# Products of constants in the plan's waits, before the feed-forward of a fused attention, Fourier and feed-forward kernel

## The chip, the cores and the metric

The kernel runs on one core of a Trainium2 chip. A core has a matrix engine (TensorE, in the profile PE, with its weight loads as PEld), a vector engine (VectorE, DVE), an engine for elementwise functions (ScalarE, ACT), a general one (GpSimd, POOL) and SyncE (SP), from whose queue most transfers are sent. Each engine runs its own list of instructions in order and waits for the others through semaphores. PE writes its results to PSUM, which has eight banks; DVE and ACT read them there. The metric is the device time of one execution in microseconds (us), the median of the runs.

## What is computed

The input is q, k and v of 8 batches, 8 heads, 576 positions and 64 features, and two weight matrices, w1 of 512 x 2048 and w2 of 2048 x 512.

```python
scores = where(block_i >= block_j, q @ k.T / sqrt(64), -1e9)   # blocks of 64 positions
attn = softmax(scores)                                         # per batch and head
x = concat_heads(attn @ v)                                     # 8 x 576 x 512
mixed = real(fft(fft(x, axis=1), axis=2))
u = x + mixed
un = (u - mean(u)) / sqrt(var(u) + 1e-6)                       # over the 512 features
out = u + maximum(un @ w1, 0) @ w2
```

## The kernel before

The work is cut into *steps*. A step is a small piece of one stage: a group of matmuls on PE, and the parts on DVE, ACT, POOL or in a queue that follow from it. Generators, called lanes, give out the steps of each stage in order: loads and copies of a head (head_lane, prepare_lane), row maxima (max_lane), scores and exponentials (score_lane), products with v (value_lane, whose PSUM tile is av), the Fourier stage of a batch (transform_lane) and, as *fillers*, the two products of the feed-forward (feed_steps: first writes h, second writes acc). Side lanes load the weights and convert them to pairs of f16 (load_lane, weight_lane); this is DVE, ACT and POOL work on the tile W.

The main loop (from line 1068) is a planner that runs while the program is written. It keeps a clock of its own, `now`, and books the cost of each step, a figure in the code, on a model of each engine. `ready(step)` is the time at which a step's inputs are there by that model and, where the step needs a PSUM bank, at which a bank is free. The loop takes the next step, `issue` moves `now` to the time at which the step can start and adds its cost on PE, then it emits its matmuls; the parts on the other engines are kept in `pending` and emitted in order of their planned starts (`give`). All instructions are kept in the order in which they are emitted (`keep_in_program_order`, through `mm`, `tp` and `Ordered`), so the plan is the order on every engine, PE's too, and the chip waits only where an input is late.

PSUM is shared. One bank holds av; seven others are in three pools: three in ps, two in h, two in acc. Before the feed-forward all seven are lent to any step (`lent` holds the three names, and `rings` the time at which each bank is free by the plan). With the first filler `lent` becomes `["ps"]`: h and acc then belong to the feed-forward.

Heads of later batches are held back until the first weight's parts are there (the condition on `('w', 15)`). So the start of the kernel is the attention of batch 0, its Fourier stage, the loads and conversions of the weights, and then the first feed-forward; after that attention and Fourier steps run between the fillers.

Names that are used below: raw is a head's load, lead its rounded copy, rest the remainder of the rounding (written by DVE, POOL and a transfer); M is a head's row maximum, which DVE reduces from PSUM, PE transposes (with ident) and ACT writes to mt, which a transfer copies into lead before the scores can start; ph and pl are the exponentials as a pair of f16; DEN and x are the values' last parts on DVE; xd is x in DRAM, from which the Fourier stage is loaded. `ident` is the 128 x 128 identity in f32, loaded first on SP's queue, and `ones` a tile of 1.0, set by DVE.

```python
if i is None:
    lent = ["ps"]
    issue(filler)
```

Of the kernel before, what the change touches and what calls it, by code (L numbers as in the profile page):

```python
# [9 lines left out]
F32 = mybir.dt.float32  # L10
F32R = mybir.dt.float32r
F16 = mybir.dt.float16
# [10 lines left out]
P = 128  # L23
# [19 lines left out]
PSHIFT = 5  # L43

BANKS = {"ps": 3, "h": 2, "acc": 2}

KM = D + 8
KS = KM + 1
# [152 lines left out]
def tile_attn_fourier_ffn(  # L201
# [6 lines left out]
    ps_av = pool("ps_av", 1, space=PSUM)  # L208
    ps = {name: pool(name, n, space=PSUM) for name, n in BANKS.items()}
    dram = pool("dram", 3, space=DRAM)  # L210
# [4 lines left out]
    def mm(*args, **kw):  # L215
        return tc.keep_in_program_order(nc.tensor.matmul(*args, **kw))  # L216
# [7 lines left out]
    ident = const.tile([P, P], F32, name="ident")  # L224
# [3 lines left out]
    ones = const.tile([P, P], F32, name="ones")  # L228
# [42 lines left out]
    now = 0.0  # L271
    queues = {x: Queue() for x in "DAGQKM"}
    done = {}
    current = "ps"
    rings = {name: [0.0] * n for name, n in BANKS.items()}
    lent = list(BANKS)


# [5 lines left out]
    def ready(step):  # L284
        r = max((done[x] for x in step.after), default=0.0)
        return max(r, min(rings[x][0] for x in lent)) if step.bank else r

    def book(engine, t, cost):

        used = [queues[x] for x in {"X": "DK", "G": "GK", "P": "G"}.get(engine, engine)]  # L290
        while True:
            at = max(x.fit(t, cost) for x in used)
            if at <= t:
                return max(x.book(t, cost) for x in used)
            t = at

    pending = []
    issued = [0]

    def issue(step):  # L300
        nonlocal current, now
        t = max(now, ready(step))
        if step.cost:
            give(t)
        if step.cost:
            now = t = t + step.cost
            for x in queues.values():
                x.forget(now)
        free = None
        starts = []  # L310
        for engine, cost in step.chain:
            if engine == "B":
                free = t + HOP
            elif engine == "L":
                t = t + cost
            elif engine in scratch:

                if cost:
                    t = max(t, scratch[engine][0] - HOP)
                else:  # L320
                    scratch[engine] = sorted(scratch[engine][1:] + [t + HOP])
            else:
                t = book(engine, t + HOP, cost)
                if engine != "M":
                    starts.append(t - cost)
        t += HOP
        if step.key is not None:
            done[step.key] = t
        if step.bank:
            current = min(lent, key=lambda x: rings[x][0])  # L330
            rings[current] = rings[current][1:] + [t if free is None else free]
        parts = step.emit()
        if parts is None:
            return
        if step.cost:
            next(parts, None)
        for at in starts:
            pending.append((at, len(pending) + 1000000 * issued[0], parts))
        issued[0] += 1

    def give(t):

        soon = sorted((x for x in pending if x[0] <= t), key=lambda x: x[:2])
        pending[:] = [x for x in pending if x[0] > t]
        for _, _, parts in soon:
            next(parts, None)
# [721 lines left out]
    while True:  # L1068
# [13 lines left out]
        for w, side in enumerate(sides):  # L1082
            if side is None or not may(side) or ready(side) > until:
                continue
            engine, cost = next((x for x in side.chain if x[0] in "DAGQKXP"), (None, 0.0))
            at = max(now, ready(side))
            ahead = queues[{"X": "D", "P": "G"}.get(engine, engine)].fit(at, cost) - at if engine else 0.0
            if ahead <= AHEAD[engine in ("D", "X") and first] or at + ahead + cost + FREE <= until:
                issue(side)
                sides[w] = next(weights[w], None)  # L1090
                break
        else:
            w = None
# [5 lines left out]
        if soon:  # L1099
            i = min(soon, key=lambda i: heads[i].place)  # L1100
        elif feed and ready(filler) <= now or feed and not able:
            i = None
        elif able:
            i = min(able, key=lambda i: ready(heads[i]))
        elif any(sides):
            w = min((w for w, x in enumerate(sides) if x is not None and may(x)), key=lambda w: ready(sides[w]))
            issue(sides[w])
            sides[w] = next(weights[w], None)
            continue
        elif pending:  # L1110
            give(pending[0][0])
            continue
        else:
            assert filler is None and not any(heads)
            break
# [3 lines that stand above are left out]
            filler = None  # L1119
        else:  # L1120
            issue(heads[i])
            heads[i] = next(lanes[i], None)
# [46 lines left out]
```

## Time and profile before

| | us |
|---|---|
| median of 3 runs | 1279.11 |
| lowest and highest | 1277.9 and 1280.24 |
| span of the profiled execution | 1275.3 |
| mean granted clock of PE in it | 0.947 |

The span goes from the first to the last instruction of the profiled execution. Its own time isn't listed apart from the runs; against their median, 1279.11 - 1275.3 = 3.8 us lie around the span.

How to read its lines. A page begins with the busy time of each engine and its share of the span, then 40 equal slices of the span with the busy share in tenths. PEclk is the clock that PE was granted, in tenths of full speed. The windows view gives the same for chosen stretches: length, then busy time and count of instructions for PE, PEld, DVE, ACT and POOL, then the granted clock, the share of the transfer engines and GB/s. The timeline lists instructions by start and duration; `out<-in` are the program's names, x the count merged in a row, and brackets hold the idle time of the engine before it and what ended it. The waits view sums these idle times by what ended them (total, times, longest). The chain is the work that ended last, followed back. L216 and L219 are the helpers mm and tp, L194 that of the other engines. Matmuls are pipelined, so a row's duration is longer than the distance between two starts.

### The profile page before, as it was taken

The numbers are of one execution on the slowest core, as the hardware profiler recorded it, in microseconds if no ns is written. First come the engines' busy times: TensorE is split into PE (matmuls) and PEld (weight loads), VectorE is DVE, ScalarE is ACT, GpSimd is POOL, SyncE is SP. The second block draws the span as 40 slices with busy tenths as digits, with TensorE's granted clock in tenths as the row PEclk, the third lists the DMA queues.
The fourth block names the chain that finished last, engine by engine and source line by source line (L and its number), as shares of the span: only waits on it lengthen the run. The fifth ranks groups of instructions, "written<-read, shape, count | busy, mean of one in ns | idle before, by whom it ended". The sixth has DMA issues, their size and how long they took to land.

```text
span 1275.3 us, 25121 instructions
## 1 busy us (share of the span) xinstructions
PE 1181.1 (93%) x10068; PEld 892.9 (70%) x10068; DVE 703.5 (55%) x1433; ACT 548.7 (43%) x1137; POOL 523.6 (41%) x593
## 2 busy tenths in 40 slices
PE   5772598999799999999999999999999999999998
PEld 5672376677677777777777777777777667766665
DVE  6787777756747574664546573557445414422211
ACT  5655647554444555534645545454443112111110
POOL 4664944454643654563534644446441400300000
PEclk9655688999899999999999999999999999999999
DMA  7674242342223233232323232413220100000000
GB/s 210 201 243 156 80 140 70 87 111 52 74 71 109 62 81 86 79 75 54 93 75 95 65 90 68 111 51 87 77 74 10 40 19 19 21 17 1 17 17 17
DMA packets 56371, 99.07 MB, mean 78 GB/s; under 512 B 7757, under 2 KB 26653, under 8 KB 56256
## 3 DMA queue, kind: packets, MB, share of 16 engines
q1 hardware_dynamic: 49152, 73.16, 21.2%
q10 hardware_dynamic: 4384, 16.78, 4.0%
q0 software_dynamic: 2720, 7.54, 2.1%
q8 instruction: 79, 1.29, 0.4%
q14 instruction: 36, 0.29, 0.1%
HBM read 58.46 MB, written 18.87 MB: 61 GB/s over the span
## 4 chain that ended last, share of the span: by engine, by line
PE 80%; DVE 10%; POOL 3%; issue 3%; DMA 2%; ACT 1%; SPq 0%; DVEq 0%; POOLq 0%; ACTq 0%
PE acc L216 28%; PE h L216 27%; PE ps L216 17%; PE av L216 6%; DVE W L194 2%; DVE M L194 2%; DVE tmp L194 2%; PE ps L219 2%; POOL u L194 1%; DMA lead<-mt 1%; DVE VL L194 1%; POOL W L194 1%; POOL pl L194 1%; DVE rest L194 1%; POOL ag L194 0%
## 5 line engine op out<-in xcount | busy, mean ns | idle before, releaser
L216 PE MATMUL h<-uh,W 128*128 128x256 f16 x2304 | 431.4, 275 | 2.7 <-DVE M L194 2.3
L194 POOL TENSOR_TENSOR pl<-p,ph 128x288 f16<-128x288 f32 (+1 forms) x256 | 253.7, 1002 | 355.6 <-ACT p L194 167.8
L216 PEld LDWEIGHTS <-W 128*128 128x128 f16 x3456 | 325.8, 99 | 64.9 <-issue 6.3
L216 PE MATMUL acc<-W,gh 128*128 128x512 f16 x1104 | 329.8, 380 | 0.0
L216 PE MATMUL h<-ul,W 128*128 128x256 f16 x1152 | 315.8, 274 | 0.0
L194 DVE TENSOR_REDUCE M<-ps 128x1 f32<-128x448 f32 (+3 forms) x292 | 131.9, 484 | 181.3 <-PE ps L216 180.5
L194 ACT ACTIVATE gh<-h 128x512 f16<-128x512 f32 x138 | 82.3, 597 | 305.1 <-PE h L216 302.3
L216 PE MATMUL ps<-lead 72*128 72x64 f32 (+9 forms) x700 | 201.3, 346 | 9.2 <-ACT lead L194 6.8
L216 PE MATMUL acc<-W,gl 128*128 128x512 f16 x552 | 209.2, 379 | 0.0
L194 DVE SCALAR_TENSOR_TENSOR gl<-h,gh 128x512 f16<-128x512 f32 x138 | 94.6, 687 | 200.9 <-ACT gh L194 200.8
L194 ACT ACTIVATE ph<-ps 128x512 f16<-128x512 f32 (+1 forms) x233 | 117.5, 506 | 146.9 <-PE ps L216 144.3
L216 PEld LDWEIGHTS <-gh 128*128 128x128 f16 x1104 | 96.7, 98 | 80.1 <-issue 4.7
L216 PEld LDWEIGHTS ps<-lead 72*128 72x128 f32 (+1 forms) x700 | 128.0, 202 | 18.3 <-ACT lead L194 6.8
L216 PEld LDWEIGHTS <-ph 128*128 128x128 f16 x1920 | 113.5, 104 | 31.1 <-ACT left L194 4.9
L216 PE MATMUL ps<-rest 128*128 128x320 f32 (+3 forms) x350 | 124.0, 361 | 1.4 <-ACT p L194 0.8
L216 PE MATMUL av<-VH,ph 128*128 128x65 f16 x960 | 118.1, 203 | 6.1 <-DVE x L194 6.1
L194 ACT ACTIVATE p<-ps 128x512 f32<-128x512 f32 (+1 forms) x233 | 117.2, 505 | 4.3 <-POOL pl L194 2.8
L216 PE MATMUL av<-VH,pl 128*128 128x65 f16 x960 | 116.6, 201 | 1.8 <-POOL pl L194 1.4
L216 PE MATMUL av<-VL,ph 128*128 128x64 f16 x960 | 117.2, 201 | 0.0
L194 POOL TENSOR_TENSOR rest<-raw,lead 64x576 fp32r<-64x576 f32 x64 | 96.9, 1514 | 15.1 <-ACT lead L194 9.5
L216 PEld LDWEIGHTS <-gl 128*128 128x128 f16 x552 | 54.0, 98 | 66.2 <-DVE gl L194 1.7
L216 PEld LDWEIGHTS <-pl 128*128 128x128 f16 x960 | 94.8, 103 | 2.7 <-POOL pl L194 2.5
(169 smaller groups left out, 1435.4 us busy)
## 6 DMA issues: line engine op xcount, KB each, us to landing
raw<-in_qk_dram SPq DMA_DIRECT2D x64, 288.0 KB
rest<-lead SPq DMA_DIRECT2D x128, 144.0 KB
W<-in_moe_w_ch_dram ACTq DMA_DIRECT2D x14, 1024.0 KB
V<-in_v_dram SPq DMA_DIRECT2D x32, 320.0 KB
xd<-x SPq DMA_DIRECT2D x32, 256.0 KB
out_dram<-u SPq DMA_DIRECT2D x32, 256.0 KB
u<-xd SPq DMA_DIRECT2D x8, 512.0 KB
u<-in_moe_w_ch_dram ACTq DMA_DIRECT2D x4, 512.0 KB
```

What stands on the lines that cost most here:

```text
L194: x = f(*args, **kw)
L216: return tc.keep_in_program_order(nc.tensor.matmul(*args, **kw))
L219: return tc.keep_in_program_order(nc.tensor.transpose(*args, **kw))
```

## The change

A tile of the pool acc is taken at the beginning and kept; the plan counts one bank fewer in that pool. In `issue`, as long as more than one pool is lent (before the first filler), each step that has a cost on PE is preceded by `keep_busy` with the time that the plan would let PE wait before it: 4.8 products for each microsecond, rounded down. A product has a 128 x 128 block of ones' bits as weights and 256 columns of ident's bits, both read as f16, and goes to the kept tile, which nothing reads. Every product starts and stops its own sum.

```diff
 BANKS = {"ps": 3, "h": 2, "acc": 2}
+
+IDLE_RATE = 4.8
...
-    rings = {name: [0.0] * n for name, n in BANKS.items()}
+    rings = {name: [0.0] * (n - (name == "acc")) for name, n in BANKS.items()}
...
+    idle = ps["acc"].tile([P, 512], F32, name="acc")
+
+    def keep_busy(us):
+
+        for _ in range(int(us * IDLE_RATE)):
+            mm(idle[:, 0:256], ones.bitcast(F16)[:, 0:P], ident.bitcast(F16), start=True, stop=True)
+
     def issue(step):
         nonlocal current, now
         t = max(now, ready(step))
         if step.cost:
             give(t)
+            if len(lent) > 1:
+                keep_busy(t - now)
         if step.cost:
             now = t = t + step.cost
```

## The prediction

> **What bounds the kernel now.** I read the page first, its busy shares and its 40 slices.
>
> ```profile
> PE 1181.1 (93%) x10068; PEld 892.9 (70%) x10068; DVE 703.5 (55%) x1433; ACT 548.7 (43%) x1137; POOL 523.6 (41%) x593
> PE   5772598999799999999999999999999999999998
> PEclk9655688999899999999999999999999999999999
> ```
>
> PE (TensorE) is the bound of the whole, but not of its start. A slice is 31.9 us; in the first five PE is half to three quarters busy and its clock is mostly granted at half. From the seventh on PE is full at the full clock, so whatever the start saves or loses moves everything behind it by as much. The question is what the start would gain from a faster PE. The windows view cuts it where the timeline of PE shows its waits; the first feed-forward product, which ends the time in which the change acts, stands at 164.23.
>
> ```profile
> 0.00:164.23 164.23, 96.89 (x687) 82.78 (x688) 127.00 (x226) 96.83 (x192) 104.23 (x114) 0.67 0.59 179
> 0.00:18.36 18.36, 5.12 (x17) 3.91 (x18) 12.51 (x38) 5.75 (x9) 5.49 (x10) 1.00 0.89 242
> 18.36:36.35 17.99, 17.99 (x139) 16.34 (x140) 14.23 (x24) 14.69 (x31) 12.16 (x12) 1.00 0.53 145
> 60.88:69.50 8.62, 8.62 (x78) 8.17 (x79) 2.71 (x9) 6.45 (x14) 5.88 (x7) 0.50 0.83 251
> 69.50:96.81 27.31, 19.21 (x170) 17.45 (x167) 25.46 (x42) 15.32 (x31) 16.01 (x16) 0.56 0.78 244
> 96.81:115.13 18.32, 0.00 (x1) 0.00 (x1) 13.68 (x20) 10.73 (x20) 12.72 (x13) 0.50 0.75 257
> 139.48:157.71 18.23, 6.73 (x29) 4.88 (x29) 13.06 (x23) 11.89 (x24) 17.89 (x22) 0.64 0.27 81
> 157.71:164.23 6.52, 6.09 (x58) 5.32 (x58) 5.08 (x10) 4.28 (x9) 6.09 (x8) 0.50 0.53 150
> 212.86:1275.30 1062.44, 1042.97 (x9010) 774.96 (x9007) 542.44 (x1141) 426.03 (x893) 399.22 (x462) 1.00 0.22 61
> ```
>
> The columns are the stretch, its length, busy time and count of PE, PEld, DVE, ACT and POOL, then clock, DMA share and GB/s. Two stretches are full of PE work (18.36 to 36.35 and 60.88 to 69.50); 69.50 to 96.81 belongs to DVE, 25.46 of 27.31 us; in 96.81 to 115.13 PE does nothing; 139.48 to 157.71 belongs to POOL, 17.89 of 18.23.
>
> The 1.00 of the first two rows can't be right. In the timeline the same three products of the values step follow each other at 23 us half as fast as at 183 us:
>
> ```profile
> 23.18 0.24 PE L216 MATMUL av<-VL,ph 128*128 128x64 f16 x1
> 23.89 0.24 PE L216 MATMUL av<-VH,pl 128*128 128x65 f16 x1
> 183.29 0.19 PE L216 MATMUL av<-VL,ph 128*128 128x64 f16 x1
> 183.69 0.19 PE L216 MATMUL av<-VH,pl 128*128 128x65 f16 x1
> ```
>
> Each pair spans 13 starts: 0.71 / 13 = 0.055 us against 0.40 / 13 = 0.031. So 23 us is cold too, and the clock column starts with no record. The start is then nearly all cold: of its 96.89 us of PE work about half would go at the full clock, some 48 us. That is no gain yet: what counts is who waits for PE. The waits of DVE between 16 and 97 us:
>
> ```profile
> DVE DEN L194 <- PE av L216: 4.0, 2, 3.5
> DVE M L194 <- PE acc L216: 4.0, 1, 4.0
> DVE vacc L194 <- PE ps L216: 2.1, 1, 2.1
> DVE x L194 <- DMA xd<-x: 1.9, 1, 1.9
> DVE M L194 <- PE ps L216: 0.8, 1, 0.8
> DVE M L194 <- PE h L216: 0.5, 1, 0.5
> ```
>
> DVE waits 4.0 + 4.0 + 2.1 + 0.8 + 0.5 = 11.4 us for PE. More than that can't be won before 97 us, since DVE's instructions keep their order.
>
> **The change, part by part.** *What one product costs.* The feed-forward's first products have the same shape (128x128 weights, 256 moving f16 columns), cold at 164 us and warm at 300 us:
>
> ```profile
> 164.40 0.42 PE L216 MATMUL h<-ul,W 128*128 128x256 f16 x1
> 168.24 0.40 PE L216 MATMUL h<-ul,W 128*128 128x256 f16 x1
> 299.94 0.27 PE L216 MATMUL h<-ul,W 128*128 128x256 f16 x1
> 301.25 0.27 PE L216 MATMUL h<-ul,W 128*128 128x256 f16 x1
> ```
>
> One in three is a ul product, so 3.84 us hold 18 starts, 0.213 us each, and 1.31 us hold 12, 0.109 each. At 4.8 for each microsecond that the plan would wait, products fill 4.8 x 0.213 = 102% of the planned wait when cold and 52% when warm.
>
> *Does this raise the clock?* Four neighbouring windows show both directions:
>
> ```profile
> 165.07:168.49 3.42, 3.42 (x18) 2.36 (x17) 3.42 (x3) 0.00 (x0) 3.04 (x4) 0.50 0.02 5
> 168.49:171.90 3.41, 1.08 (x10) 0.82 (x9) 3.38 (x7) 1.75 (x3) 0.00 (x0) 1.00 0.92 237
> 171.90:175.31 3.41, 3.41 (x18) 2.37 (x17) 2.21 (x6) 0.00 (x0) 0.00 (x0) 0.50 0.25 100
> 175.31:178.73 3.42, 3.42 (x32) 3.11 (x31) 2.14 (x4) 2.27 (x4) 0.00 (x0) 1.00 0.02 4
> ```
>
> A cold stretch of 3.41 us full of such products is followed by the full clock, twice; a warm one with 1.08 us of work is followed by half the clock. So a planned wait of a few microseconds warms PE, and a wait that is longer than planned, or than twice its products, cools it again. The Trainium skill, "TensorE: Matmul & The Clock Gate", Part 1, says the same of a free-running window of about 3.4 us, and that one idle window puts the clock back to half; the rows above agree. By that rule alone, which speaks against the change, the products help only where work follows them within a window, and the sum would shrink to the case "warm in the waits and cold in the work" below, 1279.
>
> *How many products.* PE idles 164.23 - 96.89 = 67.3 us before the feed-forward: 67.3 x 4.8 = 323 if the plan waits as long as the chip does. If it counts its work at the full clock (48.4 us) and takes as long, it waits 115.8 us: 556. Both ends stay open.
>
> *The first wait.* The plan's own figures for the first head's load and copy are 0.25 + 0.6 + 0.25 + 1.0 + 2.0 + 0.25, then 0.25 + 1.15 + 0.25, in all 6.0: 28 products. They read ident, whose load is issued first.
>
> ```profile
> 0.73 0.39 SPq L194 DMA_DIRECT2D ident<-in_c_id_dram  x1
> 5.58 1.15 ACT L194 CAST lead<-raw 64x1152 fp32r<-64x1152 f32 x1 [3.57 <-DMA raw<-in_qk_dram]
> 6.79 1.65 PE L216 MATMUL ps<-lead 72*128 72x64 f32 x5 [6.79 <-ACT lead L194]
> 11.64 6.67 DMA lead<-mt
> ```
>
> No row shows when ident lands: after 0.73 + 0.39 = 1.12, and before 5.58, when the raw tile, sent later on this queue, had landed. With 28 x 0.213 = 6.0 us cold the first real product moves from 6.79 to between 7.1 and 11.6, +0.3 to +4.8. From the middle of the bounds, 3.3, the cold run ends at 9.3; a full window of products (on the mean after one and a half, 5.1 us, at 8.4) halves its rest, so 8.9, +2.1, and the work behind it, 1.65 us for the first five, then runs warm, -0.6 or so: **+1.5 us**. Behind it the mt transfer (6.67 us) is waited for in any case, so nothing hides the delay, unless that transfer's end is set by other transfers; the lower end becomes 0.
>
> ```profile
> 28.74 0.22 DVE L194 TENSOR_SCALAR DEN<-av,vacc 128x5 f32<-128x5 f32 x1 [0.52 <-PE av L216]
> 42.00 5.75 DMA lead<-mt
> 51.95 0.49 DVE L194 TENSOR_REDUCE M<-acc 128x1 f32<-128x320 f32 x1 [4.01 <-PE acc L216]
> ```
>
> *18.36 to 36.35.* PE is full; up to 28.74 us, where the row of DEN stands, DVE waits 2.1 + 0.8 + 0.5 = 3.4 us for it. From 18.36 to 28.74 are 10.4 us of cold work, behind the first mt transfer, in which the clock may fall. With a first 5.1 us cold (a window and a half) the rest takes 2.7, so 7.8; products of planned waits inside it add some 0.5: **-2.0**, bounds -3.4 and +5 (next part's slower rival).
>
> *47.8 to 52.* DVE's 4.0 us for M: PE starts there at 47.8, when another mt transfer ends (42.00 + 5.75), and works 4.2 us, cold. At the full clock -2.1, if still cold 0: **-1.0**.
>
> *60.88 to 69.50.* DVE's 3.5 us for av would halve, but then it waits for the xd transfer (1.9 us now, longer then), which PE doesn't set. Left is half of the later wait and a little: **-0.5**, bounds 0 and -3.5. What is late next is DVE itself, 25.46 of 27.31 us.
>
> *96.81 to 157.71.* Up to 115 PE waits for the transfers and folds of the first mirror, so its 18.32 x 4.8 = 88 products, 18.7 us if all were cold, fit; if the wait were gone they would cost just these. Later POOL sets the pace. **0**, with -2 if the few PE steps in between were on the path.
>
> *The feed-forward's start.* From 157.71 to 164.23 PE is busy 6.09 us, cold; warm it would be through 3.0 us earlier, and its own first 4.26 us (164.23 to 168.49) 2.1 us earlier. But then PE waits until DVE's M, behind DVE's W:
>
> ```profile
> 168.49:171.41 2.92, 0.59 (x5) 0.38 (x4) 2.89 (x6) 1.48 (x2) 0.00 (x0) 1.00 0.90 240
> 170.49 0.88 DVE M L194 x3
> 171.41 6.08 PE h L216 x39
> ```
>
> DVE is busy 2.89 of those 2.92 us; most of the 5.1 is lost there. **-1.5**, bounds 0 and -5.
>
> *The bank.* The plan may hold six banks instead of seven at once before the feed-forward, so a step can be given out later or in another order. No row prices it; the nearest are the M reductions that free banks: one or two of the DVE waits above could come back, up to +4, and another order can gain as well, to -3. I take 0.
>
> Sum: +1.5 - 2.0 - 1.0 - 0.5 + 0 - 1.5 + 0 = -3.5. The profiled span is 1275.3, the median 1279.11, so 3.8 us lie around the span; I take them as unchanged. Span 1271.8, time **1275.6**.
>
> **The rivals.** *Hidden anyway, or warm in the waits and cold in the work* (25%): DVE, POOL and transfers set the start (25.46 of 27.31, 17.89 of 18.23), and the clock falls in the transfer waits. Then the second to fourth terms shrink to -1.5 and the first stays: 1279.1 + 1.5 - 1.5 = 1279.
>
> *Products in the way* (18%), slower. In the two stretches where PE has no idle time, 17.99 + 8.62 = 26.6 us, the plan, at the full clock, may see half as waits: 13.3 x 4.8 = 64 products, 13.6 us cold. With a share w of that time warm, work and products take 40.2 x (1 - w/2); below 26.6 only if w is over 0.68. At w = 0.35 it is 33.2, +6.6: 1285.7. For it: the mt waits just ahead of such work. Against: products are dense and warm PE in one or two windows.
>
> *The clock doesn't answer to constants* (5%): then 67.3 / 0.213 = 316 products fit into the idle time, and each one more costs 0.213; with 440, +26: 1305.
>
> *DVE's waits vanish* (10%): -8 of its 11.4, -5 at the feed-forward, +1.5: 1267.6.
>
> **How the numbers follow.** My forecast (1271 to 1276.5) has 42%. Of this kernel a measurement tells about 0.2%, 2.6 us. Faster: 42 + 10 = 52%; same 25%; slower 18 + 5 = 23%. The range, 1267 to 1285, leaves out the constants' case, the worse half of products in the way, and an edge of the last case. The likeliest case's own range is 1271 to 1276.5.
>
> **What would show it.** In the changed profile: a group of products on ident and ones, 323 to 556 of them, all before the first h product; the values step's starts 0.031 apart in the first 100 us, and the granted clock of 38 to 93 us far over 0.5; the first lead product near 8.9; DVE's waits for PE before 97 us at 6 to 8 instead of 11.4; the first h product near 160. It is wrong if these starts stay 0.055 apart while PE has no idle time left (slower), or if they are 0.031 apart and the stretch without PE work still starts at 96.8 and the first h product stands at 164.2 (same).

## The result: 0.28% slower

| | before | after |
|---|---|---|
| median of 6 runs each, side by side | 1279.88 us | 1282.95 us |
| lowest and highest | 1277.9 and 1280.47 | 1280.94 and 1284.14 |
| ratio, with its 95% interval | | 1.0028 (1.0017 to 1.0038) |
| profiled execution, its span | 1275.3 us | 1280.1 us |
| mean granted clock in it | 0.947 | 0.979 |

The change is 3.1 us slower; 1275.6 us was forecast, with a chance of 52% that it would be faster. The clock did what was forecast and the time did not follow. The page of the changed kernel, its busy shares and 40 slices:

```profile
PE 1217.3 (95%) x10650; PEld 920.0 (72%) x10650; DVE 706.3 (55%) x1433; ACT 545.4 (43%) x1137; POOL 526.2 (41%) x593
PE   8886788899999999999999999999999999999998
PEclk9987889899999999999999999999999999999999
```

The first five digits of PE were 57725 and are 88867, PEclk went from 96556 to 99878. 10650 - 10068 = 582 products were added. In the groups by line, in the timeline and in the windows of the changed kernel (the helper mm is now L218, tp L221, that of the other engines L196):

```profile
L218 PE MATMUL acc<-ident,ones 128*128 128x256 f16 x582 | 82.7, 292 | 2.6 <-DMA ident<-in_c_id_dram 2.6
2.58 5.38 PE L218 MATMUL acc<-ident,ones 128*128 128x256 f16 x28 [2.58 <-DMA ident<-in_c_id_dram]
7.71 0.93 PE L218 MATMUL ps<-lead 72*128 72x64 f32 x5
24.70 0.19 PE L218 MATMUL av<-VH,ph 128*128 128x65 f16 x1
25.12 0.19 PE L218 MATMUL av<-VH,pl 128*128 128x65 f16 x1
38.00:93.00 55.00, 47.73 (x510) 40.08 (x509) 44.84 (x85) 32.23 (x71) 36.37 (x35) 0.91 0.85 234
178.62 0.40 PE L218 MATMUL h<-uh,W 128*128 128x256 f16 x1 [3.54 <-DVE M L196]
```

The 28 products of the first wait start at 2.58; the first lead product starts at 7.71, 0.92 us later than before. The two rows of the values step are 14 starts apart: 0.42 / 14 = 0.030 us, the warm distance. Between 38 and 93 us the clock is 0.91; the same window of before:

```profile
38.00:93.00 55.00, 43.88 (x372) 39.49 (x372) 44.11 (x81) 32.30 (x69) 36.33 (x37) 0.51 0.79 239
```

But the first h product stands at 178.62 instead of 164.23. That row alone says little, since the plan now gives out other work ahead of it. To compare kernels with different orders, I count the columns of all matmuls except the products, and ask when equally much is still to be done (the last start with at least so much left):

| PE work left, us at full clock | before, at us | after, at us | after minus before |
|---|---|---|---|
| 1000 | 69.4 | 63.6 | -5.8 |
| 992 | 120.6 | 120.3 | -0.3 |
| 950 | 213.0 | 213.1 | +0.1 |
| 850 | 341.3 | 340.3 | -1.0 |
| 660 | 553.5 | 560.3 | +6.8 |
| 10 | 1260.9 | 1265.7 | +4.8 |

Between these rows the difference swings (up to +9.5 at 930 left), since the two orders do the same work in another sequence, and each row is of one execution. Two things are to be explained: a lead of 5.8 us at 64 us that is gone at 120, and a lag that arises behind 340 us, where there is no product any more. PE's waits behind 340 us, first before, then after:

```profile
PE ps L219 <- DVE M L194: 1.5, 1, 1.5
PE av L216 <- POOL pl L194: 1.2, 1, 1.2
PE ps L216 <- DVE M L194: 0.6, 1, 0.6
PE ps L219 <- DVE zc L194: 0.2, 1, 0.2
```

```profile
PE av L218 <- DVE x L196: 2.0, 1, 2.0
PE ps L221 <- DVE M L196: 1.6, 1, 1.6
PE ps L218 <- DVE M L196: 1.5, 3, 0.6
PE av L218 <- POOL pl L196: 0.8, 2, 0.6
PE ps L218 <- ACT fs L196: 0.6, 1, 0.6
PE ps L218 <- PE ps L218: 0.2, 1, 0.2
```

They sum to 3.5 and 6.7 us. The wait of 2.0 us for x has a consequence in the windows, before and after:

```profile
520.00:540.00 20.00, 20.00 (x173) 15.02 (x172) 13.88 (x27) 13.61 (x32) 8.84 (x9) 1.00 0.18 47
```

```profile
520.00:540.00 20.00, 18.00 (x153) 14.28 (x152) 14.34 (x30) 12.93 (x31) 8.38 (x9) 0.91 0.18 47
```

PE is idle for 2.0 us and its clock falls to 0.91 of the window besides: 0.09 x 20 = 1.8 us more. So 3.2 + 1.8 = 5.0 of the 5.8 us that are lost between 340 us and the end come from waits that the order of before does not have. The part of the clock is not there each time: six kernels of this document have this order and this wait of 2.0 us, and the clock falls behind it in three of their profiles (this one, the bank alone, the changed kernel with the later conversion) and not in the other three.

### The profile page after: what moved, and what is told of

Read it like the earlier page. It is cut to its first block, busy times and chain, and to the rows that moved or that the text cites. A ratio compares the mean times of both kernels' runs of the same rounds, so it can differ in the third digit from the quotient of the medians.

```text
span 1280.1 us, 26277 instructions
## 1 busy us (share of the span) xinstructions
PE 1217.3 (95%) x10650; PEld 920.0 (72%) x10650; DVE 706.3 (55%) x1433; ACT 545.4 (43%) x1137; POOL 526.2 (41%) x593
## 4 chain that ended last, share of the span: by engine, by line
PE 81%; DVE 8%; DMA 4%; POOL 3%; ACT 2%; issue 1%; SPq 0%; DVEq 0%; ACTq 0%; POOLq 0%
PE acc L218 29%; PE h L218 28%; PE ps L218 16%; PE av L218 6%; DVE W L196 3%; DVE M L196 2%; PE ps L221 2%; DMA raw<-in_qk_dram 1%; DMA lead<-mt 1%; POOL pl L196 1%; DMA xd<-x 1%; DVE rest L196 1%; DVE un L196 1%; DVE VL L196 1%; POOL W L196 1%
## 5 line engine op out<-in xcount | busy, mean ns | idle before, releaser
L218 PE MATMUL h<-uh,W 128*128 128x256 f16 x2304 | 431.7, 274 | 5.9 <-DVE M L196 3.5
L196 POOL TENSOR_TENSOR pl<-p,ph 128x288 f16<-128x288 f32 (+1 forms) x256 | 261.1, 1033 | 336.4 <-ACT p L196 159.9
L218 PEld LDWEIGHTS <-W 128*128 128x128 f16 x3456 | 325.3, 99 | 69.3 <-DVE M L196 3.8
L218 PE MATMUL acc<-W,gh 128*128 128x512 f16 x1104 | 330.3, 381 | 0.0
L218 PE MATMUL h<-ul,W 128*128 128x256 f16 x1152 | 315.2, 274 | 0.0
L196 DVE TENSOR_REDUCE M<-ps 128x1 f32<-128x192 f32 (+2 forms) x289 | 129.1, 481 | 166.6 <-PE ps L218 166.6
L196 ACT ACTIVATE gh<-h 128x512 f16<-128x512 f32 x138 | 82.2, 596 | 311.3 <-PE h L218 307.2
L218 PE MATMUL acc<-W,gl 128*128 128x512 f16 x552 | 209.5, 379 | 0.0
L196 DVE SCALAR_TENSOR_TENSOR gl<-h,gh 128x512 f16<-128x512 f32 x138 | 94.6, 687 | 194.1 <-ACT gh L196 193.7
L218 PE MATMUL ps<-lead 72*128 72x64 f32 (+9 forms) x701 | 193.1, 334 | 8.1 <-DVE M L196 5.0
L196 ACT ACTIVATE ph<-ps 128x288 f16<-128x288 f32 (+1 forms) x236 | 118.2, 504 | 143.9 <-PE ps L218 142.6
L218 PEld LDWEIGHTS <-gh 128*128 128x128 f16 x1104 | 96.3, 99 | 80.2 <-issue 4.2
L218 PEld LDWEIGHTS ps<-lead 72*128 72x128 f32 (+1 forms) x701 | 121.6, 192 | 18.4 <-issue 2.9
L218 PE MATMUL ps<-rest 128*128 128x288 f32 (+2 forms) x353 | 122.7, 356 | 2.7 <-DVE M L196 2.5
L218 PEld LDWEIGHTS <-ph 128*128 128x128 f16 x1920 | 104.4, 98 | 25.2 <-issue 4.0
L196 ACT ACTIVATE p<-ps 128x288 f32<-128x288 f32 (+1 forms) x236 | 118.0, 503 | 3.4 <-POOL pl L196 3.3
L218 PE MATMUL av<-VH,ph 128*128 128x65 f16 x960 | 108.5, 195 | 4.0 <-DVE x L196 4.0
L218 PE MATMUL av<-VH,pl 128*128 128x65 f16 x960 | 107.1, 194 | 2.6 <-POOL pl L196 2.4
L218 PE MATMUL av<-VL,ph 128*128 128x64 f16 x960 | 108.0, 193 | 0.0
L196 POOL TENSOR_TENSOR rest<-raw,lead 64x576 fp32r<-64x576 f32 x64 | 96.2, 1503 | 16.4 <-ACT lead L196 12.0
L218 PEld LDWEIGHTS <-gl 128*128 128x128 f16 x552 | 54.0, 98 | 66.0 <-DVE gl L196 1.0
L218 PEld LDWEIGHTS <-pl 128*128 128x128 f16 x960 | 88.9, 98 | 3.9 <-POOL pl L196 3.2
```

Of the source, the lines that this page charges most:

```text
L196: x = f(*args, **kw)
```

## The experiments

All ratios are to the kernel before, run in the same session. Medians moved by up to 4 us between sessions (before: 1278.32 to 1282.16), so only ratios are compared across them.

### The bank without the products, and the products without the bank

```diff
# the bank alone: the plan after the change, no kept tile, no product
-    idle = ps["acc"].tile([P, 512], F32, name="acc")
...
-            if len(lent) > 1:
-                keep_busy(t - now)
```

> The changed kernel's plan (one bank fewer) without a single product; every engine has the changed kernel's order. Theory A, the other order costs and the products gain: slower than the changed kernel, 1284 to 1290 us, first feed-forward product at 178 or later. Theory B, the order is neutral and what the warm clock wins is lost again to transfers: 1278 to 1282. Theory C, the products themselves stand in the way: about 1280, the time before.

Measured: 1287.08 us, ratio 1.0059 (1.004 to 1.0078), within theory A. Its order is that of the changed kernel on every engine, and no bank is kept, so nothing but the order differs from before. PE's waits behind 340 us include the same 2.0 for x and 1.6 for M (the profiled execution, 1291.91 us, is the slowest of the six):

```profile
...
PE av L218 <- DVE x L196: 2.0, 1, 2.0
```

The order that follows from one bank fewer is slower without any product. With the products the ratio was 1.0028, in another session; that the products won the difference back did not show again below (1.0008 without them, 1.0005 with them).

```diff
# the products alone: before's plan; they go to the bank that the step is about to take
+    products = [0]
     def ps_tile():
-        return ps[current].tile([P, 512], F32, name=current)
+        t = ps[current].tile([P, 512], F32, name=current)
+        for _ in range(products[0]):
+            mm(t[:, 0:256], ones.bitcast(F16)[:, 0:P], ident.bitcast(F16), start=True, stop=True, skip_group_check=True)
+        products[0] = 0
+        return t
...
+            products[0] = int((t - now) * 4.8) if len(lent) > 1 and step.bank else 0
```

> The order of before with all seven banks; before each step that takes a bank the same number of products goes into the bank that the step is about to overwrite. Theory A: 1272 to 1277, the first feed-forward product at 158 to 163. Theory B: 1278 to 1281, with the values step's starts at 0.031 us but the last x before the Fourier stage still at 96 to 98 us. Theory C: 1282 to 1285.

Measured: 1284.58 us, ratio 1.0049 (1.0026 to 1.0072), with 416 products and a clock of 0.969. It lies in theory C's range, products in the way, and was a surprise: the lead over before is 3.7 us at 66 us and 0.8 at 120, and at 162 us it is a lag of 5.4, which is 6.6 from 341 us to the end. The place of the loss, between 120 and 162 us, shows in the timeline of DVE and POOL, first before, then with the products:

```profile
144.92 0.95 DVE L194 TENSOR_SCALAR W<-W 128x1024 int32<-128x1024 int32 x1
...
146.43 3.37 POOL L194 TENSOR_TENSOR u<-u,add 128x255 f32<-128x255 f32 x2
```

```profile
145.44 5.96 DVE L194 TENSOR_SCALAR W<-W 128x1024 int32<-128x1024 int32 x1
145.81 0.72 POOL L194 TENSOR_TENSOR u<-u,dif 128x257 f32<-128x257 f32 x1
146.50 1.40 POOL L194 TENSOR_TENSOR u<-u,add 128x255 f32<-128x255 f32 x2
148.59 2.25 POOL L194 TENSOR_TENSOR W<-p,W 128x512 f16<-128x512 f32 x2
```

The same DVE instruction (the shift for the 13th weight piece) took 0.95 us in one and 5.96 in the other. Where it is short, POOL's neighbours are stretched (3.37 instead of 1.40 us); where it is long, POOL runs on at its own pace and DVE ends 0.6 us after POOL's list is through (148.59 + 2.25 = 150.84; 145.44 + 5.96 = 151.40). One keeps the other out. In the changed kernel it took 4.85 us too, and as much with the bank alone, without a product.

### Four transfers fewer

The second suspect for the lost lead was the transfers. In the changed kernel and in before, four of the 18 weight transfers (the fifth to the eighth) are left out, so those weights are whatever stood in the tile.

```diff
-        scalar.dma_start(raw(x).rearrange("p (j n) -> p j n", j=n), weight(i, n))
+        if not 4 <= x < 8:
+            scalar.dma_start(raw(x).rearrange("p (j n) -> p j n", j=n), weight(i, n))
```

> The changed kernel without the fifth to eighth of the 18 weight transfers (4 of 18 MB; the weights' values are then others, the instructions on all other engines and their order are the same). Theory B: the wait of 9.4 us for the raw tile at 69 us shrinks to 4 to 5, and the last x before the Fourier stage (96.3 us in the changed kernel) comes at 86 to 91. Theories A and C: raw still waited for, x at 94 to 97.

> The kernel before without the same four transfers. Theory B: the cold PE and DVE hold the start here, so the last x before the Fourier stage moves from 97.4 us to 93 or later, by less than in the changed kernel. Theories A and C: both kernels move by the same, 0 to 2 us.

Measured: 1281.53 us, ratio 1.0023 (1.0007 to 1.0039), and 1283.59 us, ratio 1.0022 (1.0006 to 1.0038). In the changed kernel the loss stays, and the last x of the first batch ends at 99.0 us with fewer transfers, not at 86 to 91 as the theory of the transfers (B) had it. That it ends at 96.8 in the profile with all transfers says little: in the two kernels below that are the same up to there it ends at 101.8 and 106.7. In before it ends 2.4 us earlier (95.5 instead of 97.9), but in its profile the DVE instruction above took 5.95 us, and three of its ten runs lie at 1279 to 1280 us and seven at 1283 to 1286. So the meeting of DVE and POOL goes one way or the other without any product; that the two groups of runs are its two outcomes is argued, since one run of a kernel is profiled.

### Without the meeting, by leaving work out

In four kernels the conversion of the 13th weight piece on DVE is replaced by a memset to 1.0, so two of the 32 weight tiles hold a constant: before, the changed kernel, the products alone, and the bank alone.

```diff
-        vector.tensor_scalar(t, r[:, 1], 3, 0x3FFFFFFF, op0=ALU.logical_shift_left, op1=ALU.bitwise_and)
+        if x == 12:
+            vector.memset(t.bitcast(F32), 1.0)
+        else:
+            vector.tensor_scalar(t, r[:, 1], 3, 0x3FFFFFFF, op0=ALU.logical_shift_left, op1=ALU.bitwise_and)
...
-        vector.scalar_tensor_tensor(t, r[:, 0], 29, t, op0=ALU.logical_shift_right, op1=ALU.bitwise_or)
+        if x != 12:
+            vector.scalar_tensor_tensor(t, r[:, 0], 29, t, op0=ALU.logical_shift_right, op1=ALU.bitwise_or)
```

> The kernel before; the three DVE instructions that convert the thirteenth weight piece (W at 145 us) are replaced by one fill with 1.0, so two of 32 weight tiles are ones. That shift on W took 0.95 us in the profile of before and 5.96, 5.95 and 4.85 in three others, while POOL ran one instruction after the other. Theory D (which of the two engines gets in first decides some 5 us of the start): times within 3 us of each other, 1275 to 1278, against 1276.3 to 1282.6 for before. If D is wrong: 1278 to 1282 with the same spread.

> The changed kernel with the same fill in place of that conversion. Theory D: 1278 to 1281, spread within 3 us; it stays 1 to 5 us slower than the kernel before with the fill, by the order of one bank fewer. If the products themselves cost the time, it stays slower than the order alone with the fill, which the changed kernel isn't without it.

> The order of before, with products in each step's own bank, with the same fill. Theory D: what the products win comes through: 1 to 5 us faster than the kernel before with the fill, 1271 to 1276. If products stand in the way: 2 us or more slower than it.

> The order of one bank fewer, without products, with the same fill. Theory D: 1282 to 1285, 3 to 5 us above the same order with products.

| no conversion of the 13th piece | before's order | the order with one bank fewer |
|---|---|---|
| without products | 1278.79 us, 0.9985 (0.9961 to 1.0008) | 1283.76 us, 1.0008 (0.9993 to 1.0024) |
| with products | 1279.09 us, 0.9977 (0.9958 to 0.9995) | 1283.28 us, 1.0005 (0.9985 to 1.0025) |

Down the columns (products) the ratio moves by 0.0008 and 0.0003, which can't be told from nothing; along the rows (order) by 0.0023 and 0.0028, 5.0 and 4.2 us between the medians (the products are 416 on the left and 582 on the right). Three expectations of theory D failed. In before's order the products were to win 1 to 5 us, and the medians differ by 0.3 us the other way; in the other order the kernel without products was to be 3 to 5 us slower than with them, and is 0.5 us slower. And the spread of the runs did not shrink, it was 6 to 11 us on this chip, before's own 10. The meeting at 145 us is therefore not the only thing that differs from run to run; what else does is open.

### Other orders

Is it the bank, or is any other order slower? One kernel takes the bank from the pool h instead of acc; one keeps all seven banks and changes a figure of the plan.

```diff
# one bank fewer in h
-    rings = {name: [0.0] * n for name, n in BANKS.items()}
+    rings = {name: [0.0] * (n - (name == "h")) for name, n in BANKS.items()}
```

```diff
# another figure
-HOP = 0.25
+HOP = 0.26
```

> The kernel before, but its plan has one bank fewer in the pool h instead of acc before the feed-forward; no product, no kept tile. PE's, DVE's, ACT's, POOL's and SP's lists are all in another order than before's. Theory K (a bank fewer is what costs, whichever it is): it costs what the kernel with the bank of acc alone cost, +4 to +8 us against before, ratio 1.003 to 1.006. Theory O (only the order that the plan happens to give decides): another value than that, anywhere from -5 to +8 us, and the part of it that arises behind 340 us, where all banks are as before, is 3 us or more of it, either way.

> The kernel before with seven banks and no product; one figure of the plan, the hop from engine to engine, is 0.26 us instead of 0.25, which gives another order on every engine and changes nothing else. Theory K (the bank is what costs): within 2 us of before, 0.9985 to 1.0015. Theory O (the order decides): 3 us or more away from before, to either side, ratio at or over 1.0023 or at or under 0.9977, with 3 us or more of lag or lead made behind 340 us.

Measured: 1292.7 us, ratio 1.0116 (1.0101 to 1.0131), and 1309.49 us, ratio 1.0244 (1.0231 to 1.0257). The second has no bank fewer and no product, and is 31 us slower than before. "The bank itself costs" falls; the order decides, and by more than the 8 us that were expected at most. In the profiles 5.0 and 19 us of the lag arise behind 340 us, the rest ahead of that. PE's longest waits behind 340 us in the kernel with the other figure:

```profile
PE ps L216 <- DVE M L194: 7.0, 7, 2.1
PE ps L216 <- ACT p L194: 4.0, 4, 2.1
```

These two sums alone are 11.0 us, against 3.5 for all of before's (the profiled execution, 1319.08 us, is the slowest of its six). All three other orders tried were slower; that is too few to say how an order is distributed, but enough to say that before's is a good one, and that a change of it is not free.

### Another operation for the shift

> The kernel before, in its own order; the shift of the 13th weight piece, the DVE instruction that took 0.95 us in before and 4.85 to 5.96 us in four other profiles while POOL worked through its list, is made by another DVE operation (scalar_tensor_tensor with a column of masks) of which no row shows such a stretch. Theory S (DVE and POOL exclude each other in that kind of instruction and whoever comes first decides some 5 us): the instruction takes 1.0 to 1.5 us whatever POOL does, POOL's two instructions there are not stretched, the first h product stands at 161 to 165 us, and the time is -1 to -3 us against before, ratio 0.9977 to 0.9993. Rival (it is load of the memory, not that exclusion): the instruction is stretched to 3 us or more all the same, and the time is that of before.

> The kernel before, in its own order and with its seven banks, with products of constants ahead of the steps that take a bank, into the bank that the step is about to take, and with the other shift of the 13th weight piece. Theory S: the instruction takes 1.0 to 1.5 us, the first h product stands at 160 to 164 us, and the time is 0 to 2 us under that of the kernel with the other shift alone, ratio to before 0.9965 to 0.999. Rival (products make the start fragile in another way): the stretch or another one of 3 us or more returns behind 97 us, and the time is 1281 to 1285 us as with the products and the old shift.

```diff
+        if x == 12:
+            vector.scalar_tensor_tensor(t, r[:, 1], 3, mask.broadcast_to([P, DM * n]), op0=ALU.logical_shift_left, op1=ALU.bitwise_and)
+        else:
             vector.tensor_scalar(t, r[:, 1], 3, 0x3FFFFFFF, op0=ALU.logical_shift_left, op1=ALU.bitwise_and)
```

`mask` is a column of 0x3FFFFFFF. Measured: 1278.52 us, ratio 1.0003 (0.9995 to 1.0012), and with the products 1284.38 us, ratio 1.0053 (1.0041 to 1.0065). The instruction, in the timelines of the one and of the other:

```profile
144.77 1.49 DVE L194 SCALAR_TENSOR_TENSOR W<-W,mask 128x1024 int32<-128x1024 int32 x1
```

```profile
143.08 6.48 DVE L194 SCALAR_TENSOR_TENSOR W<-W,mask 128x1024 int32<-128x1024 int32 x1
```

The expectation failed: this operation is kept out as well, for 6.48 us. That the products cost half a per cent in before's order was seen a second time.

### The meeting moved away, nothing left out

The conversion of the 13th piece is issued with the transfer of the 14th. DVE's M reductions and the first statistics of u then come ahead of it; PE's and SP's lists stay as they were.

```diff
     def weight_load(x):
         i, n, at = LANDS[x]
+        if x == 13:
+            list(weight_single(12))
...
-                    lambda: weight_single(x), 0.0, (f"D{0.19 + 0.53 * n}"
+                    lambda: weight_single(x) if x != 12 else iter(()), 0.0, (f"D{0.19 + 0.53 * n}"
```

> The kernel before; the conversion of the 13th weight piece (three DVE instructions and ACT's square) is issued with the transfer of the 14th, so DVE's three M reductions and the first statistics of u come ahead of it, and all else keeps its order. Theory P (the products' win reaches the end once DVE and POOL don't meet): no DVE instruction on W is stretched beyond 1.5 us at 143 to 151 us, the first h product stands at 161 to 166 us, and the time is within 2 us of before. Rival Q (the products' win is lost somewhere else anyway): the same here.

> The same with the products ahead of the steps that take a bank, in before's order with its seven banks. Theory P: it is 1.5 to 3 us faster than the kernel with the later conversion alone, ratio to before under 0.999, and the first h product stands 1.5 to 3 us earlier than there. Rival Q: the lead of 3 us at 120 us shrinks to under 1 us by the first h product without DVE's W, and the time is within 1 us of the kernel with the later conversion alone, or slower.

> The changed kernel with the same later conversion. Its order is another one than before's from the first heads on. Theory P and the reading that the order costs 4 to 6 us: 1279 to 1283, ratio 1.000 to 1.003, with 4 us or more of the lag made behind 340 us. Rival Q: as the changed kernel, ratio 1.002 to 1.004.

Measured: before with the later conversion 1279.44 us, ratio 1.0005 (0.9996 to 1.0014); with the products in before's order 1278.84 us, 0.9998 (0.9988 to 1.0009); the changed kernel 1283.66 us, 1.0027 (1.0015 to 1.0039). With the meeting gone the products no longer cost half a per cent. But the ratio moves by 0.0007, within the noise: the 1.5 to 3 us that were expected if the lead reached the end are not seen, though the intervals leave room for a gain of up to 2.7 us. The first two have the same order of steps, so their chains can be laid side by side; without products, then with them (there mm is L222):

```profile
204.79 0.98 PE av L216 x15
...
214.22 1.31 PE acc L216 x6
216.36 1.96 PE acc L216 x9
...
249.53 1.31 PE acc L216 x6
251.38 2.64 PE h L216 x24
...
347.12 1.00 PE h L216 x9
```

```profile
202.78 0.98 PE av L222 x15
...
212.53 2.59 PE acc L222 x6
...
216.41 1.96 PE acc L222 x9
...
251.11 2.59 PE acc L222 x6
...
254.25 2.64 PE h L222 x24
...
347.30 1.00 PE h L222 x9
```

The columns are start, length, and engine, tile and line with the count. The lead is 3.0 us when the first Fourier product starts (114.89 and 111.85), 1.5 at the first h product (165.16 and 163.64) and 2.01 at the values step's 15 matmuls into av. That step has waited 4.7 us for x in both kernels, and both clocks are at half behind it. In the kernel without products the clock is back before the six acc products, which take 1.31 us; in the other it is not, they take 2.59, and at the next row both stand at 216.4. At 251.11 six acc products again take 2.59, where they take 1.31 without products, and the lead has turned into a lag of 2.87 (254.25 - 251.38); at 347 it is 0.18. The windows of the first place, without products, then with them:

```profile
200.00:222.00 22.00, 16.29 (x137) 12.66 (x137) 17.43 (x35) 15.48 (x32) 10.54 (x11) 0.77 0.30 81
```

```profile
200.00:222.00 22.00, 18.72 (x136) 14.18 (x137) 15.02 (x32) 14.60 (x28) 8.35 (x9) 0.64 0.27 71
```

The clock falls from 0.77 to 0.64 here, and from 1.00 to 0.90 between 236 and 270 us. At the second place the lead is no longer there to be blamed: both kernels meet the same wait for DVE's W at the same time (1.17 us until 246.44, 1.18 until 246.47). What differs is a grid. The changes of the granted clock in one trace lie multiples of 3.41 us apart (212.04 and 324.68 without products, 33 x 3.413 between them; 216.05, 246.77 and 253.60 with them, 9 and 2 x 3.413), and the grid lies elsewhere in each execution (0.42 us behind a multiple of 3.413 in the one, 1.01 in the other). The windows of that grid around the wait, without products, then with them:

```profile
242.76:246.18 3.42, 2.50 (x40) 2.00 (x39) 3.38 (x4) 1.83 (x4) 2.95 (x2) 1.00 0.12 19
246.18:249.59 3.41, 2.52 (x23) 1.32 (x23) 3.31 (x10) 0.53 (x1) 0.00 (x0) 1.00 0.57 155
```

```profile
243.36:246.77 3.41, 2.23 (x34) 1.64 (x29) 3.41 (x4) 1.25 (x4) 2.43 (x2) 1.00 0.24 53
246.77:250.19 3.42, 2.94 (x19) 1.46 (x18) 2.98 (x10) 0.83 (x1) 0.00 (x0) 0.50 0.52 141
```

The idle time of PE is shared by two windows in the one and falls mostly into one window in the other, with 2.23 us of work left in it, and there the clock falls. Products are not needed for it: between 236 and 270 us the clock is 0.90 as well in before with four transfers fewer, without the conversion, and with the other shift, where there is no product. What was won ahead of the feed-forward is lost at 200 to 216 us; the loss at 247 us is the chance of the grid in this execution, and nearly all of it is taken back by 347, where the clock of the kernel without products is at half for longer (0.63 against 0.85 between 322 and 345 us).

## Why the prediction was wrong

**Read rightly.** The price of a product holds, and their number (582) came out just above the two ends (323 and 556). The products warm PE: 0.91 instead of 0.51, starts 0.030 apart. The Trainium skill, "TensorE: Matmul & The Clock Gate", Part 1, was weighed in the prediction as a rule that could reduce the sum to nothing. Its second half, that one idle window puts the clock back to half, asks for more idle time than was needed here: the clock fell behind windows that were not idle, with 1.08 us of work in the prediction's own row and 2.23 us in the row at 243.36.

**The first wait: +1.5, measured +0.92.** ident landed at 2.6, between the bounds, so the products started early enough.

**The terms up to 69 us, -3.5, with the first wait -2.0.** In before's order, for which they were worked out, they are about right: the four kernels with products lead before by 2.3 to 3.7 us at 66 us. In the changed order the lead at this point is 5.8 us in this profile, and 5.1, 2.0 and 0.7 in the three other kernels with products and this order, so 5.8 is not a price. DVE's waits for PE from 16 to 97 us, which were to fall from 11.4 to 6 to 8, are these:

```profile
DVE DEN L196 <- PE av L218: 5.5, 3, 2.7
DVE vacc L196 <- PE ps L218: 3.3, 2, 1.8
...
DVE M L196 <- PE ps L218: 0.8, 2, 0.6
DVE wst L196 <- PE ps L218: 0.5, 1, 0.5
```

5.5 + 3.3 + 0.8 + 0.5 = 10.1: other waits, in another order. So the test failed although the lead came; it had taken for granted that the order stays.

**96.81 to 157.71: 0.** The lead over before is used up ahead of this stretch's DVE work, at 120 us, and it is the order that takes it, with products or without: from 64 to 120 us the bank alone goes from a lead of 0.5 to a lag of 3.6 us, and without the conversion from 0.0 to 4.7. Between 120 and 162 us the changed kernel then loses 0.3 us. What the term left out shows in before's order: where DVE's W is stretched beside POOL, 3.9 us are lost between 120 and 162 us without products (four transfers fewer) and 6.2 and 6.9 with them. In the prediction POOL's 17.89 of 18.23 us were read as "POOL sets the pace"; that DVE and POOL take these microseconds from each other was not seen.

**The feed-forward's start: -1.5.** With all else alike (the later conversion) the lead is still 2.0 us at 203 us and nothing at 216. The cover was named too early, DVE's M behind DVE's W; the lead passed it and fell behind the next wait, that for x, to the clock.

**"Whatever the start saves or loses moves everything behind it by as much."** This premise failed too. The prediction read PE as full at the full clock from the seventh slice on. Its digits there are 8 for PE and 8 for the clock, and 7 and 8 in the eleventh slice; these are the waits at 200 to 216 and 322 to 345 us where leads are lost and won. (The fourth digit, 2, isn't "half to three quarters" either.) Of 3.0 us at 112 us nothing is left at 347 in the pair with the later conversion. In the pair without the conversion 1.4 of 1.9 us are left at the end of the two profiled executions, but not in the medians.

**The bank: 0, bounds -3 to +4.** This is the step that failed. It was priced as one or two waits for a free bank ahead of the feed-forward, against a gain from another order, and put at nothing, though no row priced it. What the bank changes is the whole plan: hundreds of rows of each engine's list stand elsewhere, the last of them at 995 us (175 of SP's, 6592 of PE's). The order by itself costs 0.59% as it stands, 0.23% and 0.28% without the conversion, and 0.29% between the two kernels with products and the later conversion: some 3 to 7.5 us, and in every one of the six profiles of this order 5.5 us or more are lost against before behind 340 us, while the eight other profiles in before's order lose 0.7 at most. The measured 0.28% is about this and no more. Of the 6.6 us between +3.1 and -3.5 the order makes some 3 us or more; the rest is the lead that was booked to the end and did not reach it.

**The rivals.** "Hidden anyway" was right about the products themselves: 0.03 to 0.08% in the three pairs without the meeting, none of it clear of noise. "Products in the way" gave the right sign for another reason; in one place it does hold. In the changed kernel PE's timeline behind DVE's stretched W reads:

```profile
153.72 0.74 PE L218 MATMUL acc<-lead 72*128 72x448 f32 x1 [5.41 <-DVE M L196]
...
155.14 1.50 PE L218 MATMUL acc<-ident,ones 128*128 128x256 f16 x6
```

PE has waited 5.41 us in one place, the waits that the plan saw behind it are gone, and the products meant for them are now work. That this is why products cost half a per cent where the meeting goes against DVE is argued from these rows and from the 6.2 and 6.9 against 3.9 us above, not shown by a run.

**What stays open.** Which of DVE and POOL comes first was not controlled, only moved away; and the spread of before's runs, 3 us in the first session and 10 in another, is not explained. The half clock behind the wait for DVE's W at about 250 us, which seven of nine profiles in before's order have and two have not, is one thing that differs from run to run; that it makes the spread was not tested. No version that does all the work beat before: the best, the products with the later conversion, is at 0.9998.

## What to carry to other kernels

Where a planner writes the order, a change of a resource that it counts is a change of the whole order, and has to be priced by a run of the plan alone, without the feature. Before a gain at the start is booked to the end, look at every wait of the bound engine behind it: a lead survives only if these waits end with it and leave the clock where it was. Before a loss in one profile is put down to the change, see whether kernels without the change have it in some of theirs. Products that are to fill a wait become work when the wait moves.

## What the hardware showed that was not expected

DVE and POOL can keep each other out for more than one instruction. In the timeline of the kernel with the bank alone a shift on W of the same shape, for an earlier piece, meets no POOL instruction:

```profile
131.92 0.69 DVE L196 TENSOR_SCALAR W<-W 128x1024 int32<-128x1024 int32 x1
```

It takes 0.69 us there, and the 13th piece's took 4.85, 5.96 and, as the other operation, 6.48 us beside POOL, each time until POOL's run of instructions without a gap was through. The Trainium skill, "SBUF — State Buffer", section "Who interferes with whom", says that the two share a pair of ports by a lock, that the loser blocks fully, and that the order of issue decides, not the shape. The traces agree on the blocking (0.95 and 5.96 us for one instruction in one order of the lists). That the order of issue decides they don't show: in both of these DVE's instruction starts 0.41 us before the same POOL instruction ends (144.18 + 1.15 - 144.92 and 144.70 + 1.15 - 145.44). And the loser may not get in between one POOL instruction and the next: in the run with 5.96 us five of them, in the rows shown above, started while DVE was kept out.

A wait of 2.0 us at 528 us, far into the steady part, cost 1.8 us more through the clock in the changed kernel, and nothing more in three other kernels of its order, where the clock stays at 1.00 behind the same wait. What a short stall of PE costs depends on where it falls in the 3.41 us grid of the clock, which lies elsewhere in every execution.
